# Attention in front of a two-layer feed-forward on one core: w_out in 2 KB rows with contiguous w_in weights, batch 0's constants in another order, and a down AV that ends on partition 127

## The chip, the cores and the metric

The kernel runs on one core of one Trainium2 chip. The metric is the device time of one execution in microseconds, the median over runs. A profiled execution gives the span from the first to the last instruction and the rows quoted below; its own time is 1.8 us longer than its span.

Engines are named as in the profile: PE is TensorE (matmuls), PEld its weight loads, DVE is VectorE, ACT is ScalarE, POOL is GpSimd, SP is SyncE, which only issues transfers here. POOL also issues transfers, those that convert from 32-bit to 16-bit floats on the way.

## The reference

For 8 batches of 8 heads, 576 positions and head size 64 it computes two attentions and adds them; the sum, laid out as 4608 tokens by 512, goes through two matrices with a gate between them:

```
q_d, k_d, v_d = means of q, k, v over 4 neighbouring positions      # 144 positions
out_d     = softmax(q_d k_d^T / 8) v_d, each row repeated 4 times   # "down"
out_local = softmax over |i - j| < 4 of (q k^T / 8), times v        # "local"
x = out_d + out_local, as (4608, 512)
h = x @ w_in            # (512, 2048)
g = h * sigmoid(1.702 h)
out = g @ w_out         # (2048, 512), 32-bit floats
```

## The kernel before, in words

**Two halves, interleaved.** The feed-forward works on nine groups of 512 tokens (TG), `g` from 0 to 8. For each group `mm1` computes 16 blocks of 128 hidden units (`ffc`), each as four matmuls over the model dimension (`dmc`), with w_in as the weights and the transposed attention output `xT[dmc]` as the moving operand; ScalarE applies the gate and writes `gT`. Then `mm2` multiplies four blocks of 128 tokens by w_out, 16 matmuls each, and `store` scales the result on ScalarE and writes it out, nearly always through SP. The order is written out by hand, engine by engine: each engine runs its own list in order, and the framework puts in semaphore waits where one instruction reads or overwrites what another touches.

The attention of batch `g + 1` is cut into pieces (`attention`) that stand at fixed places among the matmuls of group `g` (`POS`, `POS_0`). Batch 0 has nothing to hide behind: its attention is a start-up of its own (L886 to L973) ahead of group 0.

**The start-up.** POOL issues k and q of batch 0 (tiles `kb`, `qb`, two quads of heads), then ten pieces of v into `vb` (`load_vb`), three pieces of w_in (columns 0 to 511, 512 to 1023, 1024 to 2047), k and q of batch 1, and w_out 0 and 1; later, in group 0, v of batch 1, w_out 2 and 3, and k and q of batch 2. A transfer issued by POOL waits until the one eight before it has landed. DVE first writes constants (`fill`), then small selector matrices (`make_off`, `make_ident`, `make_psel`, `make_bias`), then transposes k and q (L280) and sums them over four positions (L299). PE runs warm-up matmuls (`warm`), then the local scores (`scores`, L391), the down scores (`scores_d`, L436), the pooling of v (`prep_vd_pe`, L356), and the products with v: `av_local0` (L475) and `av_down0` (L488). `normalise0` divides on DVE, `transp_sum` (L526) transposes and adds both attentions on PE, and `copy_x` writes `xT`. While these run for the head pairs 0 to 3, parts of the first w_in matmuls (`part`, through `hps_mm`, L767) are put in between: after the transposes of head pair 1 those of ffc 0 and 1 with dmc 0, after head pair 2 those with dmc 1, and so on.

**The constants.** `ez` holds the exponentials of batch 0's local scores, four tiles over two buffers named `l` in the profile. In each block of 128 columns the rows of one half use 60 of their own 64 columns; the other four are 1.0, and the other half's 64 columns are 0.0. Of the zeros, two tiles are written by DVE (L128) and two by ACT (L130); the ones come from DVE (L134). `eds` holds the down exponentials (`exp_down`, L462): 432 columns used, and before 112 more, set to 1.0 (L136).

**The weights.** `load_w_out(c)` brings 512 rows of w_out. Before, each partition takes two neighbouring rows as one stretch of 4 KB, so that hidden unit 256 f + 2 i + u stands on partition i of block 2 f + u. The w_in weights of a block are taken to match, every other column of 256:

```
    w_in_v = w_in_bf.rearrange("p c (f i u) -> p c f u i", u=2, i=128)
```

**After the start-up.** In group 0, `load_v(2)` on SP is held back until w_out 3 has landed, by a copy of one element on POOL (L884). SP issues in order: ten transfers of batch 2's v (`vf`, L222), the four output stores of group 0 (L836), and `load_v4(2)` (L246), whose data POOL adds up (L328, L331) into `vd` for the down attention of batch 2 (L633).

Of the kernel before, what the change touches and what calls it, by code (L numbers as in the profile page):

```python
# [9 lines left out]
BF16 = mybir.dt.bfloat16  # L10
# [9 lines left out]
def kernel(  # L20
# [9 lines left out]
    nc = tc.nc  # L30
    B, H, S, D = q.shape
    SD = S // 4
    HP = H // 2
    NQ = H // 4
    d_model, d_ff = moe_w_in.shape
# [12 lines left out]
    persist = ctx.enter_context(tc.tile_pool(name="persist", bufs=1))  # L48
# [9 lines left out]
    w_in_bf = persist.tile([128, n_dmc, d_ff], BF16, name="w_in_bf")  # L58
# [2 lines left out]
    vbs = [persist.tile([128, 5, H, 65], BF16, name=f"vb{i}") for i in range(2)]  # L61
    vds = [persist.tile([128, 3, HP, 65], BF16, name=f"vd{i}") for i in range(2)]
    es = [persist.tile([128, 2, 304], BF16, name=f"es{i}") for i in range(4)]
    eds = [persist.tile([128, 2, 544], BF16, name=f"ed{i}") for i in range(2)]
    ez = []
    for _ in range(2):
        t = work.tile([128, 2 * (S + SD)], FP32, name="l", tag="l", bufs=2).bitcast(BF16)
        for n in range(2):
            x = t[:, 1280 * n : 1280 * n + 1280]
# [13 lines left out]
    wz = consts.tile([128, 512], BF16, name="wz")  # L83
    off = consts.tile([128, 60], BF16, name="off")
    psel = consts.tile([128, 7, 64], BF16, name="psel")
    up = consts.tile([128, 128, 4], BF16, name="up")
# [9 lines left out]
    halves = [slice(0, 64), slice(64, 128)]  # L96
# [15 lines left out]
    def fill():  # L112
        nc.vector.memset(wz, 0.0)
        nc.vector.memset(ones[:, 0], 1.0)
        nc.vector.memset(ones[:, 1], 4.0)
        for t in kdT:
            nc.vector.memset(t[:, SD:160, :], 0.0)
        for t in vbs:
            nc.vector.memset(t[:, :, :, 64:65], 1.0)
        for t in vds:  # L120
            nc.vector.memset(t[:, :, :, 64:65], 4.0)
        for t in es:
            nc.vector.memset(t[:, :, 300:304], 1.0)
        for n, t in enumerate(ez):
            for par in range(2):
                rest = t[halves[par], :, :, 64 - 64 * par : 128 - 64 * par]
                if n < 2:
                    nc.vector.memset(rest, 0.0)  # L128
                else:
                    nc.scalar.copy(  # L130
                        out=rest, in_=wz[halves[par], None, 0:320].to_broadcast([64, 2, 320])
                        .rearrange("p j (i c) -> p j i c", c=64),
                    )
                nc.vector.memset(t[:, :, :, 64 * par + 60 : 64 * par + 64], 1.0)  # L134
        for t in eds:
            nc.vector.memset(t[:, :, 432:544], 1.0)  # L136


    def make_off():
# [124 lines left out]
    def load_w_out(c):  # L264
        nc.gpsimd.dma_start(
            out=w_out_bf[:, 4 * c : 4 * c + 4, :],
            in_=bass.AP(
                tensor=moe_w_out.tensor, offset=moe_w_out.offset + c * 512 * d_model,
                ap=[[2 * d_model, 128], [256 * d_model, 2], [1, 2 * d_model]],
            ),  # L270
        )

# [209 lines left out]
    def av_down0(hp, o):  # L482
        Ed, vd, u = eds[hp // 2], vds[0], hp % 2
        for c in range(2):
            for kc in range(3):
                q0 = SD * kc + 128 * c
                for j in range(2):
                    nc.tensor.matmul(  # L488
                        o[:, j, 65 * (5 + c) : 65 * (6 + c)],
                        lhsT=Ed[64 * j : 64 * j + 48, u, q0 : q0 + 128],  # L490
                        rhs=vd[64 * j : 64 * j + 48, kc, hp, :],
                        start=(kc == 0), stop=(kc == 2),
                        tile_position=(64 * j, 0),
                    )
# [16 lines left out]
    def transp_sum(y, x):  # L511
        y = y[0]
        turns = [
            (128, 5, x[0][:, 0:231], sub(up, 0, (1, 231))),
            (128, 5, x[0][:, 231:284], sub(up, 459, (1, 53))),
            (16, 6, x[0][:, 284:348], sub(up[0:16], 0, (1, 64))),
            (128, 5, x[1][:, 3:231], sub(up, 231, (1, 228))),
            (128, 0, x[0][:, 0:3], id128[:, 0:3]),
        ]
        turns += [  # L520
            (128, i, x[i // 2 % 2][:, c + 3 : c + 117], sub(id128, 3, (61, 2), (1, 57)))
            for i, c in enumerate((0, 114, 0, 114, 228))
        ]
        turns += [(128, 4, x[0][:, 345:348], id128[:, 121:124])]
        for n, (rows, slot, to, what) in enumerate(turns):
            nc.tensor.matmul(  # L526
                to, lhsT=y[0:rows, slot, :, :], rhs=what,
                start=n in (0, 3), stop=True,
                tile_position=(0, 0),
                skip_group_check=True,  # L530
            )
        return x
# [8 lines left out]
    def sub(t, off, *dims):  # L541
        return bass.AP(
            tensor=t.tensor, offset=t.offset + off,
            ap=[list(t.ap[0])] + [list(d) for d in dims],
        )
# [213 lines left out]
            return first + [lambda hp=hp: avx1(b, hp) for hp in range(HP)]  # L759
        return first + [lambda: avx(b, (0, 1)), lambda: avx(b, (2, 3))]  # L760

    w_in_v = w_in_bf.rearrange("p c (f i u) -> p c f u i", u=2, i=128)

    def hps_mm(g, ffc, dmc, acc, cs=None):
        n = TG // 2 if g == 0 and (dmc or cs) and ffc < 11 else TG
        for c in cs or range(0, TG, n):
            nc.tensor.matmul(  # L767
                acc[:, c : c + n],
                lhsT=w_in_v[:, dmc, ffc // 2, ffc % 2, :],
                rhs=xT[dmc][:, g * TG + c : g * TG + c + n],  # L770
                start=(dmc == 0), stop=(dmc == n_dmc - 1 and (cs is not None or c + n == TG)),
            )
# [9 lines left out]
    def mm1(g, gT, steps):  # L782
        two = [PA[i][:, u, :] for i in range(3) for u in range(2)]
        bank, abreast = [PM[0], two[0], PM[1], two[2], two[4]], 4
        if g == 0:
            bank = acc[0:6] + late
        elif g == 1:
            bank, abreast = [two[0], two[2], two[1], two[3], PM[1]], 5
            bank = bank + [PM[0], two[4], two[0], two[2]] + PM[::-1] * 4
        else:  # L790
            bank = bank + bank + PM + PM + PM
        for ffc in range(n_ffc):
            for f in steps.get(ffc, ()):
                f()
            if g and ffc < abreast:
                if ffc == 0:
                    for dmcs in ((0, 1), (2,), (3,)):
                        for u in range(abreast):
                            for dmc in dmcs:
                                hps_mm(g, u, dmc, bank[u])  # L800
            elif g or ffc > 5:
                for c in (0, TG // 2) if g == 0 and ffc < 11 else (None,):
                    for dmc in range(n_dmc):
                        hps_mm(g, ffc, dmc, bank[ffc], None if c is None else (c,))
            else:
                continue
            silu(gT, ffc, bank[ffc])
# [73 lines left out]
    o, y, x = {}, {}, {}  # L881
# [16 lines left out]
    for qd in range(NQ):  # L898
        load_qk(1, qd)
    load_w_out(0)  # L900
    load_w_out(1)
    warm(14)
    make_off()
# [34 lines left out]
    for hp in range(3):  # L938
        av_local0(hp, o[hp], range(4 if hp < 2 else 0, 5))
        av_down0(hp, o[hp])  # L940
        normalise0(o[hp], y[hp], 4 if hp < 2 else 0)
# [6 lines left out]
    def part(ffcs, *dmcs):  # L948
        for dmc in dmcs:
            for ffc in ffcs:  # L950
                hps_mm(0, ffc, dmc, acc[ffc])

    def turned(hp, n):
        x = PM if n is None else [PB[n][:, u, :] for u in range(2)]
        transp_sum(y[hp], x)
        copy_x(0, hp, x)

    av_local0(3, o[3], range(5))
    av_down0(3, o[3])
    normalise0(o[3], y[3])  # L960
    turned(0, None)
# [13 lines left out]
    for g in range(n_groups):  # L975
        b = g + 1
        if g == 0:
            for i in range(5):
                load_vb(1, i)
            load_w_out(2)  # L980
            load_w_out(3)
            for qd in range(NQ):
                prep_qk(1, qd)
                reduce_qk(1, qd, "k")
                reduce_qk(1, qd, "q")
                load_qk(2, qd)
            nc.gpsimd.memset(v4[32:64], 0.0)
            load_v(2, gate=after(w_out_bf[0:1, 12, 0:1], nc.gpsimd))
        elif b < B:
            load_v4(b)  # L990
            prep_qk(b, 0)
            pool_qk(b, 0)
            if b + 1 < B:
                for qd in range(NQ):
                    load_qk(b + 1, qd)
            prep_v(b, nc.gpsimd)
            if b + 1 < B:
                load_v(b + 1)
            prep_qk(b, 1)
            if b == 2:  # L1000
                reduce_qk(b, 1, "k")
                reduce_qk(b, 1, "q")
            else:
                pool_qk(b, 1)
            prep_v4(b, nc.gpsimd)
# [39 lines left out]
```

## Time and profile before

| what | value |
|---|---|
| median of 3 runs | 318.9 us (318.48 to 320.07) |
| the profiled execution's own time | 318.97 us |
| its span | 317.2 us |
| PE busy | 306.9 us, 97% of the span |
| mean granted TensorE clock | 0.988 |
| PE at w_in's first columns of dmc 1 | 27.75 us from the span's start |
| mm2 of group 0 begins | 43.1 us |
| groups 1 to 6, one each; group 7, without attention | 32.4 us (63.32 to 95.73 the first); 27.5 us |

A row of the timeline reads: start, length, engine, line, operation, written tile, read tiles, shape, count; in brackets the engine's idle time before it and what ended that. Lengths of matmuls include the time in which results leave the array, so neighbours overlap; the distance of their starts is what one costs: 0.216 us for 512 columns at the full clock.

A "landing" is the time from the start of the issuing instruction until the data is there, and is read for a single transfer by asking for its tile in a narrow stretch. So w_in's third piece, issued at 14.30 with 13.4 us to landing, is there at 27.7.

### The profile page before, as it was taken

What the parts mean: (1) busy time and instruction counts of PE and PEld (TensorE: products, weight loads), DVE (VectorE), ACT (ScalarE), POOL (GpSimd) and SP (SyncE); (2) the same over time, 40 slices, a digit from 0 to 9 for tenths busy, and PEclk for the clock granted to TensorE, in tenths of its full rate; (3) what the DMA queues carried; (4) which work ended last, traced back from release to release, by engine and by line L of the source; (5) the groups of instructions that cost most, each with busy time, mean ns of one, the idle gap of its engine ahead of it and who ended that gap; (6) DMA issues with size and microseconds to landing.
All of it is one profiled execution on the core that took longest, in us unless ns stands there. A gap on an engine that the chain in (4) does not pass through costs nothing.

```text
span 317.2 us, 9909 instructions
## 1 busy us (share of the span) xinstructions
PE 306.9 (97%) x4308; PEld 162.1 (51%) x4308; DVE 146.8 (46%) x308; ACT 208.6 (66%) x332; POOL 151.9 (48%) x174
## 2 busy tenths in 40 slices
PE   7797999999999999999999999999999999999995
PEld 2365766845554555445545454455454544444444
DVE  6963914690398038903890289127921670000000
ACT  6683776686885589558955885688567857316611
POOL 8942390466435973499339923992398120000000
PEclk9599999999999999999999999999999999999999
DMA  7999999659925991599249923984340210011011
GB/s 121 125 204 211 179 144 215 125 189 202 207 71 176 197 194 37 147 200 190 69 141 198 197 68 117 190 168 128 104 117 0 71 68 0 25 74 35 0 66 66
DMA packets 63100, 39.96 MB, mean 126 GB/s; under 512 B 44625, under 2 KB 52945, under 8 KB 63057
## 3 DMA queue, kind: packets, MB, share of 16 engines
q0 software_dynamic: 17840, 14.95, 33.2%
q1 hardware_dynamic: 45072, 24.32, 29.6%
q8 instruction: 33, 0.54, 0.7%
q14 instruction: 11, 0.08, 0.1%
q10 hardware_dynamic: 144, 0.07, 0.1%
HBM read 44.83 MB, written 9.44 MB: 171 GB/s over the span
## 4 chain that ended last, share of the span: by engine, by line
PE 90%; DMA 6%; POOL 2%; issue 0%; ACT 0%; DVE 0%; POOLq 0%; ACTq 0%
PE pm L848 36%; PE pm L767 24%; PE pa L767 15%; DMA w_in_bf<-in_moe_w_in_dram 4%; PE pa L409 3%; PE pa L848 2%; PE pa L655 2%; DMA qb<-in_q_dram 2%; PE pa L633 2%; PE pa L436 2%; PE pm L863 1%; POOL vb L233 1%; PE pa L568 1%; POOL w_in_bf L256 0%; PE pa L556 0%
## 5 line engine op out<-in xcount | busy, mean ns | idle before, releaser
L848 PE MATMUL pm<-w_out_bf,gT 128*128 128x512 bf16 (+1 forms) x550 | 119.5, 371 | 0.0
L767 PEld LDWEIGHTS <-w_in_bf 128*128 128x128 bf16 x614 | 59.4, 98 | 64.2 <-DMA w_in_bf<-in_moe_w_in_dram 1.7
L767 PE MATMUL pm<-xT,w_in_bf 128*128 128x512 bf16 (+1 forms) x366 | 89.0, 371 | 1.7 <-DMA w_in_bf<-in_moe_w_in_dram 1.6
L848 PEld LDWEIGHTS <-gT 128*128 128x128 bf16 x604 | 57.1, 98 | 59.5 <-issue 0.7
L778 ACT ACTIVATE gT<-pm 128x512 bf16<-128x512 f32 x88 | 52.7, 603 | 41.0 <-PE pm L767 41.0
L470 DVE TENSOR_TENSOR es<-es,mask 128x600 bf16<-128x600 bf16 x28 | 16.8, 637 | 91.2 <-ACT es L447 91.1
L767 PE MATMUL pa<-xT,w_in_bf 128*128 128x512 bf16 (+1 forms) x248 | 59.0, 358 | 0.0
L831 ACT ACTIVATE osb<-pm 128x512 f32<-128x512 f32 (+2 forms) x35 | 20.3, 582 | 30.5 <-PE pm L848 28.0
L778 ACT ACTIVATE gT<-pa 128x512 bf16<-128x512 f32 x56 | 32.1, 609 | 6.4 <-PE pa L767 6.3
L725 POOL TENSOR_TENSOR xT<-xT,od 128x576 bf16<-128x576 bf16 x12 | 17.6, 1470 | 37.7 <-DVE xT L709 37.2
L709 DVE TENSOR_TENSOR xT<-n,l 128x285 bf16<-128x285 f32 (+1 forms) x96 | 28.2, 368 | 0.0
L311 POOL TENSOR_TENSOR pq<-kT 128x576 f32<-128x576 bf16 x11 | 12.7, 1158 | 30.4 <-DVE kT L280 30.4
L328 POOL TENSOR_TENSOR pq<-v 112x512 f32<-112x512 f32 x18 | 23.7, 1318 | 3.7 <-DMA v<-in_v_dram 3.7
L833 DVE TENSOR_SCALAR osb<-pm 128x128 f32<-128x128 f32 x1 | 0.3, 293 | 54.0 <-ACT osb L831 54.0
L233 POOL DMA_DIRECT2D vb<-in_v_dram x20 | 13.7, 696 | 13.7 <-DMA w_in_bf<-in_moe_w_in_dram 3.9
L280 DVE STREAM_TRANSPOSE kT<-kb 128x576 f32<-128x576 f32 x16 | 20.0, 1247 | 0.0
L280 DVE STREAM_TRANSPOSE qT<-qb 128x576 f32<-128x576 f32 x16 | 19.8, 1240 | 0.0
L462 ACT ACTIVATE ed<-pa 128x864 bf16<-128x864 f32 x16 | 14.3, 894 | 4.9 <-PE pa L436 4.9
L447 ACT ACTIVATE es<-pa 128x600 bf16<-128x600 f32 x28 | 17.2, 669 | 0.1
L704 ACT ACTIVATE l<-l 128x1440 f32<-128x1440 f32 x12 | 16.8, 1404 | 0.4
L698 ACT ACTIVATE l<-pa 128x492 f32<-128x492 f32 x24 | 12.6, 578 | 6.2 <-PE pa L655 6.2
L699 DVE COPY n<-pa 128x492 f32<-128x492 f32 x24 | 15.0, 665 | 3.0 <-ACT l L698 2.4
(121 smaller groups left out, 365.1 us busy)
## 6 DMA issues: line engine op xcount, KB each, us to landing
out_dram<-osb SPq DMA_DIRECT2D x34, 256.0 KB, 2.1
vf<-in_v_dram SPq DMA_DIRECT2D x60, 128.0 KB, 4.6
v<-in_v_dram SPq DMA_DIRECT2D x72, 96.0 KB, 3.1
kb<-in_k_dram POOLq DMA_DIRECT2D x16, 288.0 KB, 6.5
qb<-in_q_dram POOLq DMA_DIRECT2D x16, 288.0 KB, 8.5
w_out_bf<-in_moe_w_out_dram POOLq DMA_DIRECT2D x4, 512.0 KB, 13.2
vb<-in_v_dram POOLq DMA_DIRECT2D x20, 64.0 KB, 5.1
w_in_bf<-in_moe_w_in_dram POOLq DMA_DIRECT2D x2, 512.0 KB, 8.0
```

What stands on the lines that cost most here:

```text
L233: nc.gpsimd.dma_start(out=vbs[b % 2][64 * par : 64 * par + 64, i, :, 0:D], in_=bass.AP(tensor=v.tensor, offset=v[b, 0].offset + (114 * i + ...
L280: nc.vector.transpose(out=t32.rearrange("p (i c) -> p c i", c=18), in_=store[b, qd].bitcast(FP32).rearrange("p (c d) -> p c d", c=18),)
L328: eng.tensor_tensor(out=t1[0:112], in0=x[:, :, 0:2, :], in1=x[:, :, 2:4, :], op=ALU.add)
L447: nc.scalar.activation(out=es[2 * qd + u][:, :, 0:300], in_=sp[u][:, :, 0:300], func=AF.Exp, scale=inv_sqrt_d,)
L470: nc.vector.tensor_tensor(out=ev, in0=ev, in1=mask, op=ALU.mult)
L704: nc.scalar.activation(out=l, in_=l, func=AF.Exp, scale=-1.0)
L709: nc.vector.tensor_tensor(out=out, in0=sub(n, *part), in1=sub(l, *part), op=ALU.mult)
L725: eng.tensor_tensor(out=xs, in0=xs, in1=sub(od[:, u, :], 0, (1, SD), (0, 4)), op=ALU.add)
L767: nc.tensor.matmul(acc[:, c : c + n], lhsT=w_in_v[:, dmc, ffc // 2, ffc % 2, :], rhs=xT[dmc][:, g * TG + c : g * TG + c + n], start=(dmc = ...
L778: nc.scalar.activation(out=gT[:, ffc, :], in_=acc, func=AF.Silu, scale=GELU_SCALE)
L831: eng.activation(out=osb, in_=ap, func=AF.Copy, scale=1.0 / GELU_SCALE)
L848: nc.tensor.matmul(ops[t][:, c : c + wide], lhsT=gT[:, ffc, t * 128 : (t + 1) * 128], rhs=w_out_bf[:, ffc, c : c + wide], start=(ffc == 0) ...
```

## The change

It has three parts. `load_w_out` gives each partition four single rows of 2 KB, so that hidden unit 128 f + i stands on partition i of block f, and the w_in weights become 128 neighbouring columns. In `fill` all ones of the `ez` tiles are written first, four memsets over both halves, and then only 60 of 64 zero columns; the memsets of `eds` go, as its tiles shrink to 432 columns. In `av_down0` the second block of down rows starts 16 columns after the first instead of 128, so the last 16 rows arrive on partitions 112 to 127, and `transp_sum` takes them from there, as rows 96 to 127 with a piece of `up` that is zero for the first 16. Lines after `fill` move up by one, lines after `attention` by three.

```diff
-    eds = [persist.tile([128, 2, 544], BF16, name=f"ed{i}") for i in range(2)]
+    eds = [persist.tile([128, 2, 432], BF16, name=f"ed{i}") for i in range(2)]
...
             nc.vector.memset(t[:, :, 300:304], 1.0)
+        for t in ez:
+            nc.vector.memset(t.rearrange("p j i (x c) -> p (j i x) c", c=64)[:, :, 60:64], 1.0)
         for n, t in enumerate(ez):
             for par in range(2):
-                rest = t[halves[par], :, :, 64 - 64 * par : 128 - 64 * par]
+                rest = t[halves[par], :, :, 64 - 64 * par : 124 - 64 * par]
                 if n < 2:
                     nc.vector.memset(rest, 0.0)
                 else:
+                    zero = wz[halves[par], None, 0:300].to_broadcast([64, 2, 300])
                     nc.scalar.copy(
-                        out=rest, in_=wz[halves[par], None, 0:320].to_broadcast([64, 2, 320])
-                        .rearrange("p j (i c) -> p j i c", c=64),
+                        out=rest, in_=zero.rearrange("p j (i c) -> p j i c", c=60)
                     )
-                nc.vector.memset(t[:, :, :, 64 * par + 60 : 64 * par + 64], 1.0)
-        for t in eds:
-            nc.vector.memset(t[:, :, 432:544], 1.0)
...
             in_=bass.AP(
                 tensor=moe_w_out.tensor, offset=moe_w_out.offset + c * 512 * d_model,
-                ap=[[2 * d_model, 128], [256 * d_model, 2], [1, 2 * d_model]],
+                ap=[[d_model, 128], [128 * d_model, 4], [1, d_model]],
             ),
...
-                q0 = SD * kc + 128 * c
+                q0 = SD * kc + 16 * c
...
-            (16, 6, x[0][:, 284:348], sub(up[0:16], 0, (1, 64))),
+            (32, 6, x[0][:, 284:348], sub(up[96:128], 448, (1, 64))),
...
-                to, lhsT=y[0:rows, slot, :, :], rhs=what,
+                to, lhsT=y[128 - rows : 128, slot, :, :], rhs=what,
                 start=n in (0, 3), stop=True,
-                tile_position=(0, 0),
+                tile_position=(128 - rows, 0),
...
-    w_in_v = w_in_bf.rearrange("p c (f i u) -> p c f u i", u=2, i=128)
-
...
-                lhsT=w_in_v[:, dmc, ffc // 2, ffc % 2, :],
+                lhsT=w_in_bf[:, dmc, ffc * 128 : (ffc + 1) * 128],
```

## The prediction

> **What bounds the kernel now.** I read the page first, then the waits of TensorE, then the chain that ended last, then the timeline from 0 to 65 us, and last the landings of single transfers.
>
> ```profile
> span 317.2 us, 9909 instructions
> ...
> PE 306.9 (97%) x4308; PEld 162.1 (51%) x4308; DVE 146.8 (46%) x308; ACT 208.6 (66%) x332; POOL 151.9 (48%) x174
> ```
>
> TensorE is busy for 97% of the span, so the time can fall only where it stands still or where its work shrinks. The waits of TensorE (line waiting, releaser: total us, times, longest) say where it stands still:
>
> ```profile
> PE pa L391 <- DVE qT L280: 2.8, 1, 2.8
> PE pm L767 <- DMA w_in_bf<-in_moe_w_in_dram: 1.6, 1, 1.6
> ...
> PE pa L848 <- ACT ed L462: 0.4, 1, 0.4
> PE pa L436 <- ACT l L455: 0.3, 1, 0.3
> ```
>
> Nothing of size comes later than batch 0's start-up. The chain (start, length, what) tells which of these two waits sets the end:
>
> ```profile
> 3.86 6.66 DMA qb<-in_q_dram
> 10.80 2.05 POOL vb L233 x3
> 12.85 1.45 POOL w_in_bf L256 x2
> 14.30 13.40 DMA w_in_bf<-in_moe_w_in_dram
> 27.75 0.61 PE pm L767 x4
> ```
>
> Up to 27.75 us the end is set by loads, not by computing: the third w_in transfer lands at 14.30 + 13.40 = 27.70, and everything after it is TensorE back to back. A faster start-up alone would gain nothing, it would lengthen the wait at 27.75. The timeline shows how far ahead the start-up already is:
>
> ```profile
> 5.38 0.09 DVE L134 MEMSET l<- 128x40 bf16 x1 [1.47 <-ACT l L130]
> 5.47 0.49 DVE L136 MEMSET ed<- 128x224 bf16 x2
> ...
> 7.88 1.25 DVE L280 STREAM_TRANSPOSE kT<-kb 128x576 f32<-128x576 f32 x1
> ...
> 18.23 0.31 PE L356 MATMUL pm<-vb,psel 128*64 128x256 bf16 x2
> ...
> 25.70 0.45 PE L526 MATMUL pa<-id,y 128*128 128x3 bf16 x7
> ...
> 27.75 0.61 PE L767 MATMUL pm<-xT,w_in_bf 128*128 128x256 bf16 x4 [1.59 <-DMA w_in_bf<-in_moe_w_in_dram]
> ```
>
> VectorE stands for 1.47 us in the constants, waiting for ScalarE's zero copies, and starts batch 0's first transpose at 7.88, although kb landed at 1.24 + 4.3 = 5.54. TensorE is done with the transposes of hp 2 at about 26.01 (the same seven matmuls begin at 29.09 for hp 3, and the next line follows at 29.40, 0.31 later), then waits until 27.75.
>
> **Part 1, contiguous w_in weights: the wait is moved.** The instruction lists of the two builds, with their waits, hold the same TensorE instructions in the same order; three waits differ. Before, the first w_in weights of dmc 1 (for ffc 0, a stride-2 slice) wait for the second and third w_in transfers, though they need only the first. After, the weights of ffc 0 to 3 wait for the first transfer alone, ffc 4 for the second, ffc 8 for the third. Landings: 12.80 + 6.8 = 19.6, 13.55 + 9.3 = 22.9, and 27.7. ffc 4 begins 29 matmuls after the old wait, some 3.0 us by the timeline; ffc 8 began at 35.07. Even 4 us earlier both find their weights there (about 27 against 22.9; 31.1 against 27.7). So the wait of 27.75 - 26.01 = **1.74 us** goes, and nothing takes its place in w_in. The weight loads cost the same either way: L767 with stride 2 has 98 ns, L848 from contiguous gT 98 ns, both under matmuls of a 216 ns spacing. Bound: no gain, no loss.
>
> **Part 2, the constants.** With the wait gone the start-up is on the path. Removed on VectorE: the 1.47 us stall, the six-fold alternation of L128 and L134, and the two ed memsets (0.49). The new list is four memsets of 128 x 80 elements and four of 64 x 300 as 32-bit words, none of which waits; ScalarE's four copies wait once, then run on. A 128 x 80 memset is not in the trace: between 0.09 (128x40) and 0.25 (half of L136's 0.49, 128x224); I take 0.1, the nearer. The zero memsets are L128's 0.33 at 0.28 spacing. From 1.82: 4 x 0.1 + 4 x 0.28 gives 3.3, but L140 needs the iota that ends at 3.53. From L140 to the first transpose it was 7.88 - 5.88 = 2.00, so kT starts at 5.6, qT at 6.85 (qb lands at 1.92 + 4.9 = 6.8), against 8.97: 2.1 us earlier, and with it the whole VectorE row up to 17.2 (kb and qb of the second quad land at 8.25 and 10.55, before VectorE asks).
>
> What is late next: the second quad's qT is there at 13.56 - 2.1 + 1.24 = 12.7, so its scores run at 12.8 to 13.7 instead of 15.77, and its exponentials (2.71 us) end at 16.4 instead of 19.41. prep_vd_pe, though, must wait for batch 0's v. Its chunk 3 lands at 10.80 + 5.5 = 16.3. L356 therefore moves from 18.23 to 16.35 (1.88), and the 0.3 that L436 waited for ScalarE goes too, as the exponentials are done 0.9 before TensorE comes there (17.3): 2.1 to 2.2. Whether the granted clock still falls to 0.50 from 9.4 to 15.9 then matters little, since VectorE and the loads lead in that stretch. Chunk 4 lands at 16.95, needed at 17.8. From there TensorE, VectorE and ScalarE follow each other as before, all **2.1 us** earlier. With the memsets at 0.25 each kT is 0.4 later, inside that 0.9. Bounds: 0 (if something not seen holds VectorE) to 2.2.
>
> **Part 3, w_out in 2 KB rows.** Same bytes, 512 rows in place of 256 for each of four transfers. The POOL waits are unchanged: each transfer waits for the one eight before it. Issuing costs 0.80 us with w_in's shape, 0.73 with w_out's: POOL idles there, nothing. Transfer: the queue runs in order, so differences of landings are prices. Rows of 4 KB: w_out 0 2.5 us (33.3 to 35.8), w_out 1 2.7, half of w_in's third 2.4. Rows of 2 KB, the very shape that w_out gets: w_in's first 2.65 (16.95 to 19.6), second 3.25. Extra e: 0 to 0.75 us for each, taken as 0.35.
>
> The Trainium skill (DMA: Bandwidth & Descriptors, "Why small descriptors are slow (HBM only)") gives about 3 cycles of overhead for a packet beside one cycle for 32 B. By it 2 KB rows would cost 2 x 67 cycles against 131, an estimate of 2% or 0.06 us; the sum would not change.
>
> Who waits, with TensorE 3.84 us earlier: w_out 1, landing 38.5 + 2e, is read from the ninth matmul of mm2(0), 44.87 - 3.84 = 41.0. Batch 1's v, whose last three issues wait for w_out 1, lands at 44.2 + 2e, needed about 46.05. w_out 2: 46.7 + 3e against 49.8. w_out 3: 49.7 + 4e against 55.1. The nearest is another one: L884 gates batch 2's v loads on w_out 3.
>
> ```profile
> 49.75 0.18 POOL L884 CAST vf<-w_out_bf 1x1 f32<-1x1 bf16 x1 [2.67 <-DMA w_out_bf<-in_moe_w_out_dram]
> ...
> 49.96 9.64 SPq L222 DMA_DIRECT2D vf<-in_v_dram  x10
> 65.02 0.83 SPq L836 DMA_DIRECT2D out_dram<-osb  x2
> ...
> 83.67 0.73 POOL L331 TENSOR_TENSOR vd<-pq 112x256 bf16<-112x256 f32 x1
> ...
> 85.02 0.26 PE L633 MATMUL pa<-ed,vd 48*64 48x144 bf16 x4
> ```
>
> Behind these ten issues on SP stand the output stores, and behind them load_v4, which feeds L331, 0.62 before TensorE needs it. The stores are ready at 61.2 after; SP is free at 59.6 + 4e. A loss appears only as 4e - 1.6 - 0.62, some **4e - 2.2**: zero at 0.35, 0.8 at 0.75.
>
> **Part 4, the rest.** av_down0 keeps its instructions and shapes; the sixth slot reads 32 rows instead of 16, four matmuls of 64 columns: the column count is unchanged, nothing. The smaller ed touches no instruction.
>
> **Sum.** 1.74 + 2.1 = 3.84 us off the profiled execution's own 318.97 (span 317.2, 1.77 around it; the median of the runs shown, 318.9, is 0.07 lower): **315.2**.
>
> **Rivals.**
> (a) The start-up doesn't follow: a load or an engine keeps L356 at 18.23. Only the wait goes: 318.97 - 1.74 = 317.2. For it: the new memsets have no row, and v's chunk 3 lands just 0.05 us ahead of its use. Against: every other landing lies further ahead. Chance 0.10.
> (b) Rows decide, not bytes. If a transfer's time goes with its rows, e is 2.5, the loss is 4 x 2.5 - 2.2 = 7.8, and the time 318.97 - 3.84 + 7.8 = 322.9, slower; it decides from e = 1.5. Against: w_in's transfers of that shape. Chance 0.04.
> (c) The wait stays where it was, as with a reader that needs the third transfer anyway. Then TensorE idles from 23.9 to 27.75, and the time is 319.0. The granted clock fell to 0.50 at 9.4 after idling from 7.5, and came back at 15.9; if it falls in this gap too, half of such a stretch of 6.5 us is lost: 322.2. Against: the list of waits. Chance 0.05.
> By the Trainium skill (TensorE: Matmul & The Clock Gate, "What's actually happening") an idle window of about 3.4 us halves the clock, and the window runs freely. The trace agrees in kind, with 1.9 us of idle sufficing at 7.5 and 1.74 not at 26. By that rule (c) would be on its slower end.
>
> **How the numbers follow.** The forecast has 0.77; 0.04 is left for what I don't see. Its own range is 314.4 (all bounds at their best, 4.2 with ScalarE's small waits at 24.6, and scatter of the runs, 318.48 to 320.07) to 316.1 (e at 0.75). With (a) the range is 314.4 to 317.3. Half a percent, 1.6 us, is about what a measurement of this kernel can tell from no change. Faster by more: the forecast and two thirds of (a), 0.84. Within: the rest of (a), half of (c) and others, 0.08. Slower: 0.08.
>
> **What would show it.** In the changed profile: no wait of VectorE in the constants, kT near 5.6, qT near 6.85; L355 (the old L356) near 16.4; no wait for w_in before L764; ffc 8 near 31.2; the later groups shifted by one constant; w_out landings of 2.7 to 3.3 us. It would be wrong if a TensorE wait on w_out, vb or vd of over 1 us appeared, or if the first L764 after hp 2's transposes began later than 25 us.

## The result, and the profile after

| | us |
|---|---|
| after, median | 315.06 (314.92 to 316.29) |
| before beside it, median | 318.85 (318.48 to 320.07) |
| ratio | 0.9883, 95% interval 0.9847 to 0.9919 |
| profiled execution: own time, span | 315.19, 313.4 |
| predicted | 315.2, range 314.4 to 317.3 |

The profiled execution is 318.97 - 315.19 = 3.78 us shorter than that of before; 3.84 was forecast. In a later comparison, where before itself took longer (below), the same kernel gave 316.02 (315.23 to 316.96), ratio 0.9855 [0.9797, 0.9913].

First the head of the page after:

```profile
span 313.4 us, 9902 instructions
...
PE 305.3 (97%) x4308; PEld 161.6 (52%) x4308; DVE 146.3 (47%) x302; ACT 208.5 (67%) x332; POOL 152.0 (49%) x174
```

The waits of TensorE after (total, times, longest):

```profile
PE pa L435 <- DVE qdT L298: 1.2, 1, 1.2
PE pm L731 <- DVE wz L113: 1.2, 1, 1.2
PE pa L390 <- DVE qT L279: 1.1, 1, 1.1
PE pa L845 <- ACT ed L461: 0.4, 1, 0.4
PE pm L525 <- issue: 0.2, 1, 0.2
```

The wait for w_in is gone, and the one for qT shrank from 2.8 to 1.1. The first three end before v arrives, and the 0.4 at L845 stood in the profile of before as well (there L848). The last one is new; "issue" is time in which TensorE waited for nothing that the profile shows. The chain after (start, length, what) has

```profile
5.75 3.36 POOL vb L232 x5
9.11 5.97 DMA vb<-in_v_dram
```

where before it ran through w_in to 27.75. By this chain the start-up hangs on batch 0's v, and from 15.1 on nearly all of the chain is TensorE. Another bound ends almost together with v, as e8 below shows. VectorE's timeline after:

```profile
1.78 0.40 DVE L125 MEMSET l<- 128x80 bf16 x4
2.18 1.54 DVE L130 MEMSET l<- 64x300 uint32 x4
3.75 0.22 DVE L139 TENSOR_TENSOR dm<-dm 128x60 f32<-128x60 f32 x1
...
6.17 1.25 DVE L279 STREAM_TRANSPOSE kT<-kb 128x576 f32<-128x576 f32 x1
```

No bracket, so no wait in the constants. kT starts 1.71 us earlier than before (7.88). TensorE's timeline after:

```profile
15.89 0.30 PE L355 MATMUL pm<-vb,psel 128*64 128x256 bf16 x2
...
21.37 0.32 PE L525 MATMUL pm<-id,y 128*128 128x114 bf16 x4 [0.23 <-issue]
...
23.43 0.45 PE L525 MATMUL pa<-id,y 128*128 128x3 bf16 x7
23.74 0.60 PE L764 MATMUL pm<-xT,w_in_bf 128*128 128x256 bf16 x4
```

The pooling of v's chunk 3 stands 2.34 us earlier than before (18.23), and the first dmc-1 weights 4.01 earlier (27.75), with nothing between the transposes and them. At 21.37 a run of seven transposing matmuls is cut in two. That costs 0.4 us: the row behind it begins at 21.55 here, and at 21.16 in e12 (below), where the rows from 20.38 on start at the same times and no stop follows. Last, the place where the w_out rows could have cost something (timeline after, POOL and PE):

```profile
51.65 0.18 POOL L881 CAST vf<-w_out_bf 1x1 f32<-1x1 bf16 x1 [3.60 <-DMA w_out_bf<-in_moe_w_out_dram]
...
81.09 0.26 PE L632 MATMUL pa<-ed,vd 48*64 48x144 bf16 x4
```

The gate opens 1.90 us later than before (49.75), and yet TensorE's down attention starts 3.93 us earlier (85.02): the delay was absorbed. The last piece of the chain starts at 306.28 against 310.08, 3.80 earlier: one shift, made before 24 us and carried to the end.

### The profile page after: what moved, and what is told of

Read it like the earlier page. It is cut to its first block, busy times and chain, and to the rows that moved or that the text cites. A ratio compares the mean times of both kernels' runs of the same rounds, so it can differ in the third digit from the quotient of the medians.

```text
span 313.4 us, 9902 instructions
## 1 busy us (share of the span) xinstructions
PE 305.3 (97%) x4308; PEld 161.6 (52%) x4308; DVE 146.3 (47%) x302; ACT 208.5 (67%) x332; POOL 152.0 (49%) x174
## 4 chain that ended last, share of the span: by engine, by line
PE 93%; POOL 2%; DMA 2%; ACT 1%; issue 1%; DVE 0%; POOLq 0%; ACTq 0%
PE pm L845 37%; PE pm L764 25%; PE pa L764 15%; PE pa L408 3%; PE pa L845 2%; PE pa L654 2%; PE pa L435 2%; PE pa L632 2%; DMA vb<-in_v_dram 2%; PE pm L860 1%; POOL vb L232 1%; PE pa L567 1%; PE pa L474 1%; PE pa L525 0%; PE pa L555 0%
## 5 line engine op out<-in xcount | busy, mean ns | idle before, releaser
L845 PE MATMUL pm<-w_out_bf,gT 128*128 128x512 bf16 (+1 forms) x550 | 119.5, 371 | 0.0
L845 PEld LDWEIGHTS <-gT 128*128 128x128 bf16 x604 | 57.0, 98 | 59.6 <-issue 0.8
L469 DVE TENSOR_TENSOR es<-es,mask 128x600 bf16<-128x600 bf16 x28 | 16.3, 616 | 88.7 <-ACT es L446 88.5
```

Source lines behind the costliest of these rows:

```text
L469: nc.vector.tensor_tensor(out=ev, in0=ev, in1=mask, op=ALU.mult)
L845: nc.tensor.matmul(ops[t][:, c : c + wide], lhsT=gT[:, ffc, t * 128 : (t + 1) * 128], rhs=w_out_bf[:, ffc, c : c + wide], start=(ffc == 0) ...
```

## The experiments

One number from each profile helps below: where the first w_in weights of dmc 1 begin, and the rest of the span behind that place. Changes to the start-up move the first; a halved clock or later waits lengthen the second.

| kernel | first dmc-1 weights | rest of the span | median of runs |
|---|---|---|---|
| before | 27.75 | 317.2 - 27.75 = 289.5 | 318.85 |
| after | 23.74 | 289.7 | 315.06 |
| after, later comparison | 23.51 | 289.9 | 316.02 |
| e1, weights and rows | 25.59 | 290.2 | 316.92 |
| e2, constants and down AV | 29.26 | 292.4 | 320.74 |
| e3, down AV | 28.12 | 291.6 | 321.36 |
| e4, w_out in 4 KB rows | 23.73 | 289.5 | 315.14 |
| e5, w_in in three tiles | 23.93 | 289.9 | 315.31 |
| e8, zero memsets later | 23.77 | 289.4 | 315.57 |
| e9, gap filled with 28 more matmuls | 30.21 | 298.6 | 330.54 |
| e10, gap filled with 18 moved ones | 30.27 | 289.5 | 319.71 |
| e11, rows of 512 B; of 256 B | 23.35; 23.35 | 290.4; 293.7 | 316.55; 320.08 |
| e12, 28 tiny matmuls | 23.36 | 295.5 | 321.2 |

The profiled execution isn't always near the median. That of e2 took 323.54 us, the longest of e2's twelve, and that of e11 with 256 B rows 318.86, 1.2 below its median.

### e1 and e2: each half alone

e1 is before with the diff's lines for `load_w_out` and `hps_mm`; e2 is before with those for `eds`, `fill`, `av_down0` and `transp_sum`.

> The kernel before with parts 1 and 3 alone: 128 neighbouring w_in columns as weights and w_out in 2 KB rows; constants and down AV as before. My theory: the wait for w_in at 27.75 goes (1.74 us), the start-up stays where it was, so the first dmc 1 weights come near 26.0 and the time is 318.9 - 1.7 = 317.2. Rival 1, all of the gain comes from the earlier start-up: no change, 318.9. Rival 2, all of it comes from the wait: 315.1.

> The kernel before with the constants and the down AV alone; stride-2 w_in weights and w_out in 4 KB rows as before. My theory: the start-up is some 2 us earlier, but TensorE then stands still from about 23.7 until the third w_in transfer lands near 27.8: no change, 318.9. If the granted clock falls in that gap of 4 us, up to 3 us more, 322. Rival 1 (the start-up alone brings the gain): 315.1 to 316.8.

e1 gave 316.92 (316.33 to 317.55), ratio 0.9892 [0.984, 0.9943]; e2 320.74 (320.14 to 323.54), ratio 1.0018 [0.9982, 1.0054]. Beside them before took 320.18 (318.16 to 322.84). In e1's timeline of TensorE the weights follow the transposes at once:

```profile
25.28 0.45 PE L526 MATMUL pa<-id,y 128*128 128x3 bf16 x7
25.59 0.60 PE L765 MATMUL pm<-xT,w_in_bf 128*128 128x256 bf16 x4
```

although the third w_in transfer landed at 15.1 + 13.8 = 28.9. The wait belonged to the way the weights were read. In e2 TensorE is done with the transposes at 23.4, a little earlier than in after (23.74, with the stop), and then waits, as the third w_in transfer lands at 14.4 + 14.8 = 29.2 in this execution:

```profile
PE pm L766 <- DMA w_in_bf<-in_moe_w_in_dram: 5.8, 1, 5.8
```

The whole gain of the start-up turned into a wait, and more: the rows of the stretches of e2 (from:to, PE busy, granted clock, DMA share, GB/s) show the clock falling in that gap,

```profile
24.00:26.00 2.00, 0.00 (x0) 0.78 1.12 210
26.00:28.00 2.00, 0.00 (x0) 0.50 1.13 215
...
30.00:34.00 4.00, 4.00 (x24) 0.50 1.12 211
34.00:38.00 4.00, 4.00 (x30) 0.83 1.52 187
```

and staying low over 6 us of work after it. That is the 292.4 in the table, 2.9 more than before's 289.5, in e2's longest execution; its median is 2.8 us lower. So the weights stand by themselves and bring 27.75 - 25.59 = 2.16 us; the constants alone bring nothing, and on top of the weights 25.59 - 23.74 = 1.85. Parts of both figures come from the clock in the start-up (see the steps below). Which of the new constants does it, the zeros without a wait or the ones in four memsets, was not tried apart.

### e3: down AV alone

Before with `q0 = SD * kc + 16 * c` and the 32-row pieces; nothing else.

> The kernel before with the down AV part alone (16 c in place of 128 c, slot 6 from partitions 96 to 127); ed keeps its 544 columns and their memsets. My theory: no change, 318.9 within 0.5; four matmuls of 64 columns as before. Rival: the row group at 96 lets these matmuls overlap others or costs a drain, a few tenths either way, not visible in the time.

321.36 (319.06 to 322.99), ratio 1.0039 [0.9998, 1.008]. No gain, and no loss that can be told from none. The rest of this profile is 2.1 us longer than before's, and 1.7 of them are its clock: w_in came at 28.1, and behind that gap the granted clock had a mean of 0.85 from 28 to 30 and 0.65 from 30 to 34 (2 x 0.15 + 4 x 0.35 = 1.7).

### e4: w_out in 4 KB rows again

```diff
-                ap=[[d_model, 128], [128 * d_model, 4], [1, d_model]],
+                ap=[[2 * d_model, 128], [256 * d_model, 2], [1, 2 * d_model]],
```

> The changed kernel with w_out in 4 KB rows again and contiguous w_in weights, so that hidden units are multiplied by other rows of w_out; only its time is read. My theory: 2 KB rows cost 0.3 us for a transfer and nothing in the end: same as the changed kernel, 315.1, with w_out 3 landing 1 to 2 us earlier. Rival: short rows bring a part of the gain (or cost one): 315.1 plus or minus 1.

315.14 (314.99 to 315.29), ratio 0.984 [0.9783, 0.9897]: the time of after. The gate on batch 2's v opened at 50.63 against 51.65, 1.02 us for four transfers, so 256 more rows cost 0.25 us for each transfer of 1 MB, and none of it reaches the end.

### e5: what made the wait

After, with w_out and the weights as before (4 KB rows, every other column), but w_in in three tiles, one for each transfer:

```diff
-    w_in_bf = persist.tile([128, n_dmc, d_ff], BF16, name="w_in_bf")
+    w_ins = [(c, persist.tile([128, n_dmc, n], BF16, name=f"w_in{c}"))
+             for c, n in ((0, 512), (512, 512), (1024, 1024))]
```

> The changed kernel with stride-2 w_in weights and w_out in 4 KB rows as before, but w_in in three tiles, one for each transfer, so that the list of waits again asks each transfer only for its own columns. My theory (the wait came from how a strided slice was set against all three transfers, not from the stride): 315.1, the same as the changed kernel, with weight loads of 98 ns. Rival: the stride itself, or the 4 KB rows, cost time: 317 to 319.

315.31 (314.83 to 317.53), ratio 0.9845 [0.978, 0.991]; first dmc-1 weights at 23.93. Weights with stride 2 load as fast as contiguous ones (98 ns) and no longer wait. e5 differs from e2 in the tiles alone, and e2 waited for 5.8 us. What waited was neither the engine nor the data: in one tile, a strided slice was taken to meet all three transfers. Contiguous slices or separate tiles both end that; the new layout of w_out is only there to let the slices be contiguous.

### e8: does VectorE bound the new start-up?

e5 with DVE's four zero memsets moved behind the last sum of q (`fill_zero()` after `reduce_qk(0, 1, "q")`).

> The three-tile kernel with VectorE's four zero memsets (1.54 us) moved behind batch 0's last sum over k and q, where VectorE waits. My theory (batch 0's v bounds the start-up): kT at 5.6 instead of 6.17, but the last v products of the start-up still begin near 15.9, so 315.0, at most 0.2 less than the three-tile kernel. Rival (VectorE's row bounds it): 0.5 less, 314.6.

315.57 (315.01 to 317.06), ratio 0.9855 [0.9785, 0.9925]. VectorE started 0.25 earlier (kT at 5.92), and the time did not fall. But the test is not clean, as TensorE then stood for v and, soon after, for the memsets that had been moved:

```profile
15.06 0.30 PE L359 MATMUL pm<-vb,psel 128*64 128x256 bf16 x2 [0.32 <-DMA vb<-in_v_dram]
...
16.85 0.42 PE L478 MATMUL pa<-vb,l 128*128 128x65 bf16 x8 [0.20 <-DVE l L140]
```

L359 is the pooling of v, L478 the local product, L140 the zeros. The other profiles say more. With the new constants the second down scores (L435) begin at 16.78 to 16.81 in six of them (after, e2, e4, both of e11, e12), wherever the pooling of v's chunk 3 stands between 15.59 and 15.94. Where v is early, they wait for the exponentials, in e2 for instance:

```profile
16.81 0.58 PE L435 MATMUL pa<-qdT,kdT 32*64 32x144 bf16 x24 [0.32 <-ACT l L454]
```

Where v is later they move with it: 16.07 gives 16.91 in the later run of after, 16.49 gives 17.33 in e5. So two bounds end almost together: v's landing, and VectorE's row with the exponentials behind it. An earlier v alone wins nothing (15.59 still gives 16.81 in e2); an earlier VectorE alone was not tried cleanly.

### e9, e10 and e12: keeping the clock up, and the price of instructions

e9 is e2 with `warm(28, t=PB[0][:, 0, :])` behind `turned(2, 2)`, in front of the waiting weights.

> The constants-only kernel with 28 warm-up matmuls (about 6 us of zeros) put ahead of the waiting w_in weights, into a bank that is free there. My theory (the gap costs twice: the wait until the third w_in transfer lands at 28 to 29, and then a halved clock): the clock stays at 1.0 and the time is 2 to 2.5 us below the constants-only kernel, near 318.3, no less. Rival (only the wait counts, the clock does nothing): the same as the constants-only kernel, 320.7.

330.54 (330.11 to 330.84), ratio 1.0305 [1.0248, 1.0363]: a miss by 12 us. The clock did stay at 1.00 from 22 to 32. But the filler ran to 30.21, 2.9 us past the landing at 14.9 + 12.4 = 27.3, and the waits of TensorE had two lines that no kernel above has:

```profile
PE pa L654 <- issue: 5.3, 6, 1.6
PE pa L408 <- issue: 2.1, 1, 2.1
```

These lie in later groups, which the edit doesn't touch. Two kernels tell apart whether the place of the filler or the number of instructions does it. e10 is e2 with `warm(14)` and `warm(4, 256)` taken out and `warm(18, ...)` put in the gap, so that TensorE has exactly e2's number of instructions; e12 is after with `warm(28, 16, ...)` behind `warm(14)`, in TensorE's free time before 8.55.

> The kernel before with the new constants and down AV alone (e2), 18 warm-up matmuls moved: the 14 at the very start and the 4 narrow ones before prep_vd_pe go, 18 of 512 columns stand between the transposes of hp 2 and the waiting w_in weights. The number of TensorE instructions is that of e2. 18 x 0.216 = 3.9 us cover 23.5 to 27.4, about where the third w_in transfer lands (27.3 to 29.2 so far). Theory (the lost clock is most of why e2 gains nothing): the granted clock stays at 1.00 in the gap and after it, where e2 had 0.50 from 26 to 34 and 0.83 up to 38, some 2.7 us of work; the time is about 318.0, by the landing 317.5 to 319. Rival (only the landing counts, the clock costs nothing): 320.7 as in e2. On e9's unexplained waits: if they came with the added instructions, TensorE has none on its own instruction stream here; if they came with matmuls at this place, some 7 us of them return.

> The changed kernel with 28 more warm-up matmuls of 16 columns right after the first 14, where TensorE waits 1.1 us for qT anyway: the same 56 added TensorE instructions as in e9, but costing no time where they stand. If e9's waits on the instruction stream (5.3 us before L654, 2.1 before L408) came from the number of instructions ahead of those places, such waits of several us appear again and the time is 318 to 323. If they came from what the 28 matmuls did at their place or from that run alone, no such wait appears and the time is 315.0 to 316.0.

e12 gave 321.2 (320.25 to 324.14), ratio 1.0041 [1.0001, 1.008], over 5 us more than after. Its start-up is as early as any (23.36), and the loss is in the rest:

```profile
PE pa L654 <- issue: 4.2, 6, 1.2
```

```profile
82.32 0.22 PE L654 MATMUL pa<-es,vb 64*64 64x57 bf16 x2
83.09 0.22 PE L654 MATMUL pa<-es,vb 64*64 64x57 bf16 x2 [0.54 <-issue]
```

The timeline shows one run of eight short matmuls cut in two; the same happens once in each of six groups. In after, L654 has no idle time at all. e10, with the filler in the gap but the count unchanged, has none either. So 56 more TensorE instructions (28 weight loads and 28 matmuls), at either of the two places tried, cost 5 to 6 us later on in e12 and some 9 in e9. No other number was tried. A queue that carries instructions brought 33 packets, 0.54 MB, in after, and 34, 0.56 MB, in e12 and e9, some 16 KB each. That these are TensorE's, that a shift of all later instructions moves the place where a packet ends, and that a dense run of short matmuls then outruns the next one, is argued, not shown.

e10 itself gave 319.71 (319.2 to 321.84), ratio 0.9989 [0.9952, 1.0026], between the two expectations. It is a blunt test of the end time, since TensorE, without the early warm-up, ran the profiled start-up at 0.50 from 20 to 26 and came to the weights at 30.27. But the clock was back at 1.00 from 28 on, and the rest is 289.5 against e2's 292.4 from a later start. The 2.9 us are the halved clock after the gap; that reading of e2's profile holds.

### e11: what rows cost

The changed kernel with w_out cut into 16 or 32 pieces for each partition:

```diff
-            out=w_out_bf[:, 4 * c : 4 * c + 4, :],
+            out=w_out_bf[:, 4 * c : 4 * c + 4, :].rearrange("p f (k n) -> p (f k) n", n=128),
...
-                ap=[[d_model, 128], [128 * d_model, 4], [1, d_model]],
+                ap=[[128, 128], [128 * 128, 16], [1, 128]],
```

(and n = 64, 32 pieces, for 256 B.)

> The changed kernel with w_out in rows of 512 B, 2048 of them for each transfer in place of 512 (hidden units are multiplied by other rows of w_out, nothing else changes). Theory (bytes decide): landings a few tenths later at most, the copy that gates batch 2's v at 51.5 to 52.5, the time 315 to 316. Rival (b) in its weak form, a price for each row, scaled from the 0.25 to 0.35 us that 256 more rows cost: 1536 more rows cost 1.8 us for each transfer, the gate moves by four times that to about 59, the loss is 7.2 - 2.2 = 5.0 us, 320. In its strong form (time as rows): four times as long, w_out 1 late for mm2(0) and over 20 us lost.

> The same with rows of 256 B, 4096 for each transfer, the row length that v already has. v's chunks of 262 KB landed 0.55 to 0.74 us apart, 2.2 to 3.0 us for 1 MB, so by the theory that bytes decide w_out costs 2.2 to 3.5 us for each transfer and the time stays at 315 to 317. By a price for each row (0.3 us for 256 rows): 4.2 us more for each transfer, 16.8 - 2.2 = 14.6 us lost, 330, with TensorE waiting for w_out in mm2(0).

Rows of 512 B gave 316.55 (315.5 to 318.28), ratio 0.9899 [0.9866, 0.9931]: the gate at 52.39, 0.74 later than with 2 KB, and no wait of TensorE for w_out. A price for each row is refuted there. Rows of 256 B gave 320.08 (318.38 to 322.15), ratio 0.9984 [0.9946, 1.0021], where bytes alone would have left 315 to 317 and a price for each row 330: both missed. w_out 1 landed at 19.6 + 22.3 = 41.9 instead of 39.4, and the waits of TensorE show it:

```profile
PE pm L845 <- DMA w_out_bf<-in_moe_w_out_dram: 2.9, 2, 1.6
```

The gate stood at 55.67, 4.0 later than with 2 KB: 1.0 us for each transfer in the mean, though w_out 1 alone took 41.9 - 37.0 = 4.9 instead of 3.1. The Trainium skill (DMA: Bandwidth & Descriptors, "Why small descriptors are slow (HBM only)") puts some 3 cycles of overhead on each packet beside one for 32 B. By it 1 MB in 256 B rows needs (11/8) / (67/64) = 1.31 times as long as in 2 KB rows, an estimate of 0.9 us on a price of 2.9; the trace agrees with its mean of 1.0. For 512 B the estimate is 0.4 and the trace has 0.74 / 4 = 0.2. Between 4 KB and 2 KB the trace has 0.25 where the rule has 0.06.

## Why the prediction was right, step by step

**The wait, 1.74.** Right in mechanism, and e1 and e5 show the mechanism by itself. In e1 the place moved by 2.16, as that execution's start-up was also 0.42 faster up to the transposes (25.59 against 26.01): its clock was halved from 11.6 to 15.0 only, before's from 9.1 to 15.9.

**The start-up, 2.1.** After minus before at the first dmc-1 weights is 4.01 = 1.74 + 2.27. The size came out, partly by luck. That the pooling of v's chunk 3 follows v's landing was right (15.84 and 15.89). The terms around it were off:

- VectorE was slower than forecast. The zero memsets took 1.54 instead of 4 x 0.28, and L139 to kT 2.42 instead of 2.00, so kT came at 6.17, not 5.6, and qT at 7.26, not 6.85. The exponentials ended at 16.74, not 16.4.
- v's chunk 3 was earlier, 10.74 + 5.1 = 15.84, not 16.3. TensorE was ready for L435 at 16.79, not 17.3. Of the slack of 0.9 that the prediction names, 0.05 was left.
- L435 thus began 2.67 earlier than before (19.46), where 2.1 to 2.2 were forecast. The stop at 21.37, which no term holds, took 0.4 back. Without v's early landing that stop would have left some 1.8.

**The clock in the start-up.** The prediction says that it matters little whether the clock falls there, since VectorE and the loads lead. This step was wrong, and the sum was spared because the clock stayed at 1.00 from 8 to 16. In before it was at 0.50 from 9.1 to 15.9 (not from 9.4: the stretch from 9 to 10 has a mean of 0.56, so 0.12 us of it at full clock). In e3, which has the old constants too, it was at 1.00 from 8 to 16. The second exponentials in before, e3 and after:

```profile
16.70 2.71 ACT L455 ACTIVATE l<-pa 64x600 bf16<-64x600 f32 x4 [1.03 <-PE pa L391]
...
15.75 2.71 ACT L455 ACTIVATE l<-pa 64x600 bf16<-64x600 f32 x4 [0.53 <-PE pa L391]
...
14.03 2.71 ACT L454 ACTIVATE l<-pa 64x600 bf16<-64x600 f32 x4 [0.53 <-PE pa L390]
```

Before and e3 start kT at 7.88 and 7.89, and yet the exponentials are 0.95 apart, and the end of hp 2's transposes 0.94 (26.01 and 25.07). So TensorE led in that stretch, and a halved clock costs some 0.9 us. Of the 2.27 us, 0.94 are before's halved clock. At an equal clock the new constants are worth 25.07 - 23.74 = 1.33 in after, and 25.07 - 23.35 = 1.72 in e11, without the stop. In before's time the halved clock doesn't show, as TensorE waited for w_in until 27.75 anyway. All profiles with the new constants have 1.00 from 8 to 16, and wait for qT for 1.0 to 2.1 us instead of 2.8; that the shorter wait keeps the clock up is argued, not shown.

**Rows of w_out, e = 0.35, loss 0.** Landings were 36.3, 39.4, 48.0 and 51.6; the price of the first two 2.6 and 3.1. Measured against e4, e is 0.25; against the landings of before the gate moved by 1.90, which makes 0.48 by the prediction's formula. Either is within 0 to 0.75, and 4e - 2.2 stays below zero. Down attention shows no loss (3.93 earlier). Most of the loss with 256 B rows came over w_out 1, which mm2(0) waited for 2.9 us (41.9, where the prediction needs it at 41.0), and not over the gate: no wait of TensorE for vd appeared. A price between that of 512 B and that of 256 B, from which the loss begins, was not tried.

**Part 4, nothing.** e3 agrees.

**The rivals.** (a) fell with L355 at 15.89. (b) in its strong form fell with e4 and with 512 B rows; a size at which rows do cost time exists, 256 B. (c), the wait that stays, didn't happen in after, but e2 is that case: start-up early, wait kept. The prediction gave it 319.0, or 322.2 with the clock falling in the gap; e2's median of 320.74 lies between, its profiled execution, in which the clock fell, took 323.54. By the Trainium skill (TensorE: Matmul & The Clock Gate, "What's actually happening") the window that halves the clock is some 3.4 us and runs freely. In e2's stretches the clock fell at about 25.1 (1.12 us of 24 to 26 at full clock make 0.78), 1.7 us after TensorE fell idle, and came back at about 35.4. These are 10.2 us apart, three such windows, as the rule has it; in before's start-up, 9.1 to 15.9, they are two. The traces add that a window need not be idle throughout: the clock fell 1.7 us after TensorE fell idle in e2, and 1.6 in before (idle from 7.5; the 1.9 of the prediction goes with its 9.4).

**What the sum did not hold.** The sum as written, 318.97 - 3.84, is 315.13; the forecast of 315.2 stands 0.07 above it, which is less than the scatter of the runs. Before itself has a cost that its profiled execution did not show. Of the 61 executions of before that were timed beside the experiments, 15 had a mean granted clock of 0.985 or less, and all of them took 321.5 us or more; the 8 with 0.998 or more took 318.2 to 320.2. After's have 0.998 to 1.00. With before's start-up the gap in front of w_in left the clock alone in one profile (before, 1.7 us) and halved it behind the gap in another (e3, 2.9 us). With the gap gone, so is that. It is the likely reason, not a shown one, why the ratio was 0.9855 in the later comparison, in which six of before's seven executions took 319.4 us or more, and 0.9883 in the first.

## What to carry to other kernels

Read what a wait waits for against what the instruction needs: here one strided slice over a tile filled by three transfers waited for the last of them, and three tiles or contiguous slices freed 1.7 us, at the same speed of loading. Find the bound of a stage before speeding it up: the earlier constants were worth nothing while that wait stood (e2) and 1.3 to 1.9 us once it had gone. Look at the granted clock before crediting a change with the whole of a shorter stage: 0.9 us of this start-up were the clock. Don't fill a gap of TensorE with added matmuls in a long program without looking at the groups behind it: 56 instructions that were free where they stood (e12) cost over 5 us elsewhere.

## What the runs showed of the hardware that was not expected

- The count of TensorE instructions ahead of a dense stretch matters: 56 more, and L654 stalls for up to 1.2 us in each of six groups (e12), 1.6 in e9; with the count unchanged (e10) not at all. A single stop of the same kind, 0.4 us at L525, stands in after and e4, without added instructions. How such stops come about stays open.
- The granted clock fell 1.6 us (before) and 1.7 us (e2) after TensorE fell idle. Behind a gap in front of w_in this cost a further 1.7 us (e3, gap of 2.9) and 2.9 us (e2, gap of 5.8); before's gap of 1.7 at 26.01 cost nothing in its profile.
- Converting transfers of 1 MB from rows of 4 KB, 2 KB, 512 B and 256 B: the gate behind four of them opened at 50.63, 51.65, 52.39 and 55.67. The step is between 512 B and 256 B.
